# Regrouping the weight conversion's calls on ScalarE and GpSimd in a fused attention and feed-forward kernel

## The chip, the cores and the metric

The kernel runs on one core of one Trainium2 chip. The metric is the device time of one launch in microseconds (us), taken as the median of several runs. Times inside the launch come from one execution recorded by the hardware profiler; they are counted from the start of its span.

## What is computed

The inputs q, k, v have 8 batches, 8 heads, 576 rows and 64 columns. The feed-forward weights `w_ch1` (512 x 2048) and `w_ch2` (2048 x 512) come out of the set-up as 64-bit floats, since they are multiplied by a 64-bit scalar. The reference, cut to what matters:

```python
scores = scale * np.matmul(q, k.transpose(0, 1, 3, 2))          # scale = 1/8
thresh = np.max(scores, axis=-1, keepdims=True) - tau
scores = np.where(scores >= thresh, scores, -1000000000.0)
attn = np.exp(scores - np.max(scores, axis=-1, keepdims=True))
attn = attn / (np.sum(attn, axis=-1, keepdims=True) + 1e-09)
x = heads_to_columns(np.matmul(attn, v))                        # (8, 576, 512)
xn = (x - mean(x)) / np.sqrt(var(x) + 1e-06) * g_ln
out = x + np.maximum(xn @ w_ch1, 0.0) @ w_ch2
```

## The kernel before, in words

**Slots and quarters.** The attention is cut into 72 slots, nine for each batch. A slot n computes the scores of one pair of heads and half of the rows (one slot of each batch takes the rows left over), their maxima on VectorE (L436), thresholds on GpSimd (`thr`, L440), exponentials on ScalarE (L450) and masked weights on VectorE (L457), and turns the weights so that they can be multiplied with v. In slots 0 to 5 the turning is done by TensorE against a diagonal (`turn_weights`). From slot 6 (`FIRST`) on, GpSimd divides the weights (L473), VectorE turns them in blocks of 32 (`turn_blocks`, L541 and L547), and SyncE sends them through a scratch tensor in DRAM (`scr`, L554 and L558) and back into `em` (L568, L572) during the next slot. The product with v (L616) uses `em` near the end of that next slot.

**Feed-forward groups.** There are 16 groups of 288 tokens. Group 0 starts in slot 6. Its steps come from a generator, and `second_part(n, i)` issues a number of them in each of the four quarters i of a slot n, by a running account of steps owed. In `first_part` each of the 16 row blocks d is four products into a PSUM tile of the tag `ff`, of which there are two buffers, followed by a relu on ScalarE (L814) that frees the buffer. A block is issued only when the weights that it needs are ready (`conversion.ended`). After one of the first relus come the square of xc (L821) and three additions on GpSimd (L823) for the variance. `second_plain` holds the second product of group 0, with copies (L853) in the place of the relus. Later groups use weights that are ready.

**The conversion of the weights.** The class `Weights` turns the 64-bit words into 32-bit floats in 32 chunks of 128 x 512; chunks 0 to 15 belong to `w_ch1`, the rest to `w_ch2`. Each chunk passes these steps:

- `fetch`: SyncE loads the raw 64-bit words into a piece of some room that is free at that time (L257).
- `begin`: two VectorE instructions make the upper bits (L273, L277). They read the high word of each pair.
- the "low" conversion: ScalarE converts the low word in place (L283).
- the "square": ScalarE squares the high word, read as a float, in place (L286). It must wait until `begin` has read that word.
- `carry`: GpSimd adds the converted low word (L296). `carry_all` does this for all begun chunks, the last one first.
- `mask`: VectorE sets tiny values to zero by the square (L302), and the piece is free again.
- `scale`: for chunks 0 to 15, GpSimd multiplies by g_ln (L312).

Two chunks are begun at the end of slot 0, and one at each of two places in slots 1 to 5. The table `BEGUN` sets this: chunks 12 to 14 are begun in the second quarter of slot 6 and 15 to 17 in the third; 18 and 19, then 20 to 22 in slot 7; 23 to 25, then 26 and 27, and 28 at the end in slot 8; 29 and 30, then 31 in slot 9.

**What sets the order.** The order of each engine's queue is the order of the calls in the program, which is written by hand (`manual_schedule`); each engine works through its queue in order. ScalarE's two instructions for a chunk are not issued by `begin`. They are kept in the list `on_scalar`, low and square alternating. `flush(1)` after each relu takes one from the list, and `flush()` in `carry_all` takes all that are left.

In a slot's order, the places that matter are, in the main loop: `mask_all` and `begin_to(masks_at)` (L1128, L1129); for slots up to 5 `carry_all` and `scale_all` (L1130 to L1132); the second quarter of feed-forward steps (L1134); `carry_all` and `scale_all` (L1135, L1136); `weights` (L1138); `mask_all` and `begin_to(behind_at)` (L1143, L1144); the third quarter (L1146); `carry_all` (L1147); the turning (L1151 or L1155). A further `scale_all` stands in `exponentials` (L446), between the two thresholds of the next slot.

Of the kernel before, what the change touches and what calls it, by code (L numbers as in the profile page):

```python
# [13 lines left out]
AF = mybir.ActivationFunctionType  # L14
# [4 lines left out]
def kernel(  # L19
# [31 lines left out]
    nc = tc.nc  # L51
# [125 lines left out]
    class Weights:  # L177
# [13 lines left out]
        def __init__(self):  # L191
            self.chunks = [
                (w1_sb[i][:, c : c + WC], w_ch1[i * 128 : (i + 1) * 128, c : c + WC], i)
                for c in range(0, DF, WC)
                for i in range(NK)
            ] + [
                (
                    w2_sb[:, m, d : d + 4].rearrange("p d c -> p (d c)"),
                    w_ch2[d * 128 : (d + 4) * 128, m * 128 : (m + 1) * 128].rearrange(
                        "(d p) c -> p d c", p=128  # L200
                    ),
                    None,
                )
                for m in range(NK)
                for d in range(0, ND, 4)
            ]
            self.n1 = NK * (DF // WC)
            self.fetched = self.begun = self.carried = self.masked = self.scaled = 0
            self.raw, self.ticks, self.on_scalar = {}, 2, []
            flat = lambda t: t.rearrange("p a b -> p (a b)")  # L210

            x_room = ffn.tile([128, NK, TOK], F32, tag="x", bufs=3, name="x_room")
            y_room = ffn.tile([128, NK, TOK], F32, tag="sq", bufs=1, name="y_room")
            stage = self.stage = consts.tile([128, 8, WC], F32, name="stage")

            n1 = self.n1
            self.free = []  # L220
            for t, n, before in (
                (w2_sb.rearrange("p m d c -> p (m d) c"), ND // 2, lambda p: n1 + 2 * p - 6),
                (hidden, 4, lambda p: 10),
                (x_room, 1, lambda p: 2 * n1),
                (y_room, 1, lambda p: 2 * n1),
                (stage, 4, lambda p: 2 * n1),
            ):
                for p in range(n):
                    self.free.append((before(p), -1, flat(t)[:, p * 2 * WC : (p + 1) * 2 * WC]))
# [37 lines left out]
        def begin(self):  # L267
            i = self.begun
            assert all(self.raw[j][0] + 6 > i or self.raw[j][0] == 10 for j in range(self.masked, i))
            self.begun += 1  # L270
            hi = self.words(i, U32)[:, :, 1]
            au = self.chunks[i][0].bitcast(U32)
            nc.vector.tensor_scalar(  # L273
                out=au, in0=hi, scalar1=3, scalar2=0x3FFFFFFF,
                op0=ALU.logical_shift_left, op1=ALU.bitwise_and,
            )
            nc.vector.scalar_tensor_tensor(  # L277
                out=au, in0=hi, scalar=0xC0000000, in1=au,
                op0=ALU.bitwise_and, op1=ALU.bitwise_or,
            )  # L280
            low, low_in, top = self.words(i, I32), self.words(i, U32), self.words(i, F32)[:, :, 1]
            self.on_scalar += [
                lambda: nc.scalar.activation(  # L283
                    low[:, :, 0], low_in[:, :, 0], func=AF.Copy, scale=2.0**-29
                ),
                lambda: nc.scalar.activation(top, top, func=AF.Square),  # L286
            ]

        def flush(self, most=99):
            while self.on_scalar and most:  # L290
                most -= 1
                self.on_scalar.pop(0)()

        def carry(self, i):
            ai = self.chunks[i][0].bitcast(I32)
# [34 lines left out]
        def carry_all(self):  # L330


            self.flush()
            for i in reversed(range(self.carried, self.begun)):
                self.carry(i)
            self.carried = self.begun

        def mask_all(self):
            while self.masked < self.carried:
                self.mask()  # L340

# [194 lines left out]
    def turn_blocks(b, s, es):  # L536


        et = att.tile([128, NB, 128], F32, tag="et", bufs=1, name="et")
        if s == HP:  # L540
            nc.vector.transpose(  # L541
                et.rearrange("p n (u c) -> p u n c", u=HP),
                es.rearrange("p u (n c) -> p u n c", c=32),
            )
        else:
            for h in range(2):
                nc.vector.transpose(  # L547
                    et[:, :, 64 * h : 64 * h + 64].rearrange("p n (j c) -> p j n c", j=2),
                    es[:, 2 * h : 2 * h + 2].rearrange("p j (n c) -> p j n c", c=32),
                )  # L550
        scr = dram.tile([4, S, 128], F32, tag="scr", name="scr")
        if b == 0:
            for a in range(4):
                nc.sync.dma_start(  # L554
                    out=scr[a].rearrange("(n r) x -> r n x", r=32), in_=et[32 * a : 32 * a + 32]
                )
            return scr
        nc.sync.dma_start(  # L558
            out=scr.rearrange("a (r n) x -> (a r) (n x)", r=32),
            in_=et.rearrange("p n x -> p (n x)"),  # L560
        )
        return scr
# [231 lines left out]
    def first_part(g):  # L794
# [6 lines left out]
        for d in range(ND):  # L801
# [10 lines left out]
                if c < NK - 1:  # L812
                    yield 1, 1
            nc.scalar.activation(hidden[:, d], p1, func=AF.Relu)  # L814
            conversion.flush(1)
            next(sums_of, None)
            yield 2, 1
            if sq is None and d and (plain or part > 1 or d == ND // 2 - 1):
# [188 lines left out]
    def at_quarter(n, i, fn, *args):  # L1007
        later_calls.setdefault((n, i), []).append((fn, args))
# [84 lines left out]
    for n in range(NS):  # L1093
# [33 lines left out]
            run_all(aside)  # L1127
        conversion.mask_all()  # L1128
        conversion.begin_to(masks_at)  # L1129
        if n <= HP + 1:  # L1130
            conversion.carry_all()
            conversion.scale_all()  # L1132
        run(n, 1)
        second_part(n, 1)  # L1134
        conversion.carry_all()  # L1135
        conversion.scale_all()  # L1136
        blocks_go = by_blocks(n)
        diags = weights(es, thr, blocks_go)  # L1138
        run_all(aside)
# [1 line left out]
        if n < SLOTS:  # L1141
            run_all(stores)
        conversion.mask_all()  # L1143
        conversion.begin_to(behind_at)  # L1144
        run(n, 2)
        second_part(n, 2)  # L1146
        conversion.carry_all()  # L1147
        box = []
        if blocks_go:
            conversion.fetch(3, wait=0)  # L1150
            scr = turn_blocks(b, s, es)  # L1151
            at_quarter(n + 1, 0, lambda b=b, s=s, scr=scr, box=box: box.append(fetch(b, s, scr)))
        else:

            made = turn_weights(s, es, diags)  # L1155
            for i, at in enumerate(
                (-1, -1, 0, 0)
            ):
                if i < 3:
                    at_quarter(n + 1, at, next, made)  # L1160
                else:
                    at_quarter(n + 1, at, lambda made=made, box=box: box.append(next(made)))
# [17 lines left out]
        second_part(n, 3)  # L1180
        conversion.begin_to(end_at)
        conversion.carry_all()
        run_all(aside)
        drip({nc.vector: 2, nc.gpsimd: 0})
    while later_calls or queue or aside or stores or drops:
# [39 lines left out]
```

## Time and profile before

| what | value |
|---|---|
| median of 3 runs | 1354.78 us (1354.15 to 1355.54) |
| the profiled execution | 1355.44 us |
| its span | 1353.6 us, 40455 instructions |
| TensorE busy | 1320.4 us, 98% |
| VectorE busy | 877.9 us, 65% |
| GpSimd busy | 630.3 us, 47% |
| ScalarE busy | 458.8 us, 34% |
| waits of ScalarE's squares (L286) for `begin` (L277), first 270 us | 10.3 + 8.8 + 4.6 + 3.3 + 1.1 us by the room of the raw words |
| waits of GpSimd's additions (L296) for the low conversions (L283), first 270 us | 16.9 + 8.2 + 7.8 + 7.0 us |

Busy times of the engines overlap, and an engine's idle time matters only where another engine waits for what comes behind it. A line of the timeline gives start, length, engine, line, operation, output and input, the number of instructions, and in brackets how long the engine stood idle before it and what ended that. The conversion's work lies in the first 172 us of the span; slots 0 to 5 take the first 78 us or so, slots 6 to 9 some 16 to 24 us each.

### The profile page before, as it was taken

How to read it: one execution, taken by the hardware profiler on the slowest of the kernel's cores; microseconds unless marked ns; L12 is line 12 of the kernel's file. 1: busy time of each engine (PE TensorE's matmuls, PEld its weight loads, DVE VectorE, ACT ScalarE, POOL GpSimd, SP SyncE). 2: the span in 40 equal slices, each digit the busy share in tenths (PEclk: the TensorE clock that was granted, in tenths of full speed). 3: DMA queues.
4: the chain of work that ended last, by engine and by line, in shares of the span. 5: the costliest groups of instructions: out<-in, count | busy, mean ns of one | idle time of the engine just before them, and what ended most of it. 6: DMA issues, size and time to landing. Idle time of an engine off the chain costs nothing.

```text
span 1353.6 us, 40455 instructions
## 1 busy us (share of the span) xinstructions
PE 1320.4 (98%) x17400; PEld 993.8 (73%) x17400; DVE 877.9 (65%) x1544; ACT 458.8 (34%) x995; POOL 630.3 (47%) x836
## 2 busy tenths in 40 slices
PE   8989899999999999999999999999999999999997
PEld 6754557869687786967778696876868677686957
DVE  7979977666755675666766667556756667666112
ACT  4865432232323323232333323233232323323120
POOL 3566655445444344444534545444444445335312
PEclk9999999999999999999999999999999999999999
DMA  8916884457644675437744476446764376343211
GB/s 159 290 39 185 216 210 148 176 155 188 182 146 146 191 194 174 151 129 192 194 141 159 138 199 182 151 146 186 188 181 152 119 195 185 125 159 128 85 18 20
DMA packets 335299, 213.94 MB, mean 158 GB/s; under 512 B 247376, under 2 KB 292688, under 8 KB 327056
## 3 DMA queue, kind: packets, MB, share of 16 engines
q1 hardware_dynamic: 329008, 210.46, 53.3%
q8 instruction: 137, 2.24, 0.7%
q10 hardware_dynamic: 5952, 0.74, 0.4%
q0 software_dynamic: 160, 0.15, 0.1%
q14 instruction: 42, 0.34, 0.1%
HBM read 124.00 MB, written 87.29 MB: 156 GB/s over the span
## 4 chain that ended last, share of the span: by engine, by line
PE 87%; SPq 1%; issue 1%; DMA 1%; DVE 0%; POOL 0%; ACT 0%; POOLq 0%; ACTq 0%; DVEq 0%
PE p L101 36%; PE seg L101 31%; PE sc L422 9%; PE sc L616 8%; PE sc L626 2%; PE var L101 1%; PE mean L101 1%; DMA em<-scr 0%; SPq L554 0%; ACT part L902 0%; SPq L118 0%; DMA k_in<-in_k_dram 0%; DVE et L547 0%; POOL w L296 0%; POOL out_dram L745 0%
## 5 line engine op out<-in xcount | busy, mean ns | idle before, releaser
L101 PE MATMUL p<-xc,w 128*64 128x288 f32 x4096 | 519.4, 409 | 9.8 <-ACT part L902 4.6
L101 PEld LDWEIGHTS p<-xc,w 128*64 128x64 f32 x4096 | 287.2, 137 | 219.6 <-issue 14.8
L436 DVE TENSOR_REDUCE neg<-sc 128x2 f32<-128x1152 f32 x144 | 188.6, 1351 | 282.4 <-PE sc L422 282.4
L473 POOL TENSOR_SCALAR e<-e,den 128x576 f32<-128x576 f32 x264 | 209.5, 805 | 133.6 <-DVE den L462 133.6
L101 PE MATMUL seg<-hidden,w 128*64 128x144 f32 x3840 | 247.9, 287 | 0.0
L101 PEld LDWEIGHTS seg<-hidden,w 128*64 128x64 f32 x3840 | 234.9, 137 | 11.5 <-issue 8.5
L457 DVE SCALAR_TENSOR_TENSOR e<-sc,thr,e 128x576 f32<-128x576 f32 x288 | 222.3, 809 | 17.3 <-POOL thr L440 11.6
L440 POOL TENSOR_SCALAR thr<-neg,low_sb 128x2 f32<-128x2 f32 x144 | 41.6, 289 | 377.7 <-DVE neg L436 376.8
L814 ACT ACTIVATE hidden<-p 128x288 f32<-128x288 f32 x256 | 106.2, 415 | 295.6 <-PE p L101 295.6
L450 ACT ACTIVATE e<-sc,neg 128x576 f32<-128x576 f32 x288 | 197.5, 754 | 2.4 <-DVE neg L436 2.4
L547 DVE STREAM_TRANSPOSE et<-e 128x1152 f32<-128x1152 f32 x118 | 161.1, 1372 | 14.3 <-POOL e L473 13.7
L422 PE MATMUL sc<-kT,qT 64*64 64x384 f32 (+3 forms) x2048 | 139.4, 403 | 3.1 <-DVE e L457 1.9
L616 PE MATMUL sc<-em,v_in 128*64 128x128 f32 (+1 forms) x2368 | 130.9, 264 | 5.2 <-DMA em<-scr 3.7
L616 PEld LDWEIGHTS sc<-em,v_in 128*64 128x64 f32 x2368 | 123.4, 138 | 14.0 <-DVE o L728 2.5
L101 PE MATMUL seg<-hidden,stage 128*64 128x144 f32 x1920 | 123.3, 286 | 0.0
L101 PEld LDWEIGHTS seg<-hidden,stage 128*64 128x64 f32 x1920 | 117.6, 137 | 2.9 <-issue 2.9
L639 ACT COPY x<-sc 128x128 f32<-128x128 f32 x120 | 31.6, 265 | 243.8 <-PE sc L422 176.0
L887 POOL TENSOR_TENSOR hidden<-hidden 128x576 f32<-128x576 f32 x60 | 84.8, 1428 | 52.0 <-ACT hidden L814 42.4
L422 PEld LDWEIGHTS sc<-kT,qT 64*64 64x64 f32 x2048 | 76.0, 133 | 44.2 <-issue 21.4
L902 ACT COPY part<-seg 128x288 f32<-128x288 f32 x74 | 29.8, 403 | 190.6 <-PE seg L101 190.1
L887 DVE TENSOR_TENSOR hidden<-hidden 128x576 f32<-128x576 f32 x60 | 51.2, 887 | 51.5 <-PE seg L101 48.5
L823 POOL TENSOR_TENSOR hidden<-hidden 128x288 f32<-128x288 f32 x48 | 38.9, 810 | 54.7 <-ACT hidden L821 52.2
(132 smaller groups left out, 1088.2 us busy)
## 6 DMA issues: line engine op xcount, KB each, us to landing
scr<-et SPq DMA_DIRECT2D x63, 1152.0 KB, 5.0
em<-scr SPq DMA_DIRECT2D x63, 1024.0 KB, 5.7
out_dram<-ot SPq DMA_DIRECT2D x248, 36.0 KB, 3.6
q_in<-in_q_dram SPq DMA_DIRECT2D x120, 72.0 KB, 2.5
er<-scr SPq DMA_DIRECT2D x132, 64.0 KB, 5.1
k_in<-in_k_dram SPq DMA_DIRECT2D x116, 72.0 KB, 2.8
v_in<-in_v_dram SPq DMA_DIRECT2D x28, 256.0 KB, 5.4
w<-in_moe_w_ch_dram SPq DMA_DIRECT2D x11, 512.0 KB, 6.5
```

The costliest lines, as they stand in the source:

```text
L101: nc.tensor.matmul(out[r], lhsT=lhsT[:, r], rhs=rhs, **flags)
L422: nc.tensor.matmul(sc[h][64 * i : 64 * i + 64, at : at + n], lhsT=ql[r] if s == HP else qT[r, half, j * 128 + 64 * i : j * 128 + 64 * i + 64],
L436: nc.vector.tensor_reduce(out=neg[:, i], in_=pairs[h], axis=AXL.X, op=ALU.max, negate=True,)
L440: nc.gpsimd.tensor_scalar(out=thr[:, i], in0=neg[:, i], scalar1=-1.0, scalar2=low_sb, op0=ALU.mult, op1=ALU.add,)
L450: nc.scalar.activation(es[:, i], blocks[i], func=AF.Exp, bias=neg[:, i : i + 1])
L457: nc.vector.scalar_tensor_tensor(out=es[:, i], in0=blocks[i], scalar=thr[:, i : i + 1], in1=es[:, i], op0=ALU.is_ge, op1=ALU.mult, accum_o ...
L473: nc.gpsimd.tensor_scalar(out=es[:, i], in0=es[:, i], scalar1=den[:, i : i + 1], scalar2=1.0, op0=ALU.mult, op1=ALU.mult,)
L547: nc.vector.transpose(et[:, :, 64 * h : 64 * h + 64].rearrange("p n (j c) -> p j n c", j=2), es[:, 2 * h : 2 * h + 2].rearrange("p j (n c) ...
L616: nc.tensor.matmul(dst[64 * h : 64 * h + 64], lhsT=vt[:, h, c, :], rhs=pick(em[:, 2 * j : 2 * j + 2, c], h), start=c == 0 and first, stop= ...
L814: nc.scalar.activation(hidden[:, d], p1, func=AF.Relu)
L823: nc.gpsimd.tensor_tensor(out=sq[:, 0], in0=sq[:, 0], in1=sq[:, c], op=ALU.add)
L887: eng.tensor_tensor(out=out[at], in0=in0[at], in1=in1[at], op=op)
```

## The change

The list `on_scalar` is split in two, `lows` and `squares`. `flush` becomes `give_scalar`, which issues from either list.

- `carry_all` issues all pending lows, then the additions. `mask_all` issues all pending squares first.
- After a relu, one pending square is issued, and only in the second quarter.
- In every slot, `carry_all` and `scale_all` now stand ahead of the second quarter's steps, and the remaining squares behind them.
- From slot 6 on, `scale_all` is also called after the second `mask_all`.
- After the third quarter all pending lows are issued. In slots 0 to 5 the additions and squares follow at once. From slot 6 on `turn_blocks` comes first, then the squares, then the additions.
- At the end of a slot squares follow `carry_all`.

```diff
@@ Weights
-            self.raw, self.ticks, self.on_scalar = {}, 2, []
+            self.raw, self.ticks, self.lows, self.squares = {}, 2, [], []
...
-            self.on_scalar += [
-                lambda: nc.scalar.activation(
-                    low[:, :, 0], low_in[:, :, 0], func=AF.Copy, scale=2.0**-29
-                ),
-                lambda: nc.scalar.activation(top, top, func=AF.Square),
-            ]
-
-        def flush(self, most=99):
-            while self.on_scalar and most:
+            self.lows.append(lambda: nc.scalar.activation(
+                low[:, :, 0], low_in[:, :, 0], func=AF.Copy, scale=2.0**-29
+            ))
+            self.squares.append(lambda: nc.scalar.activation(top, top, func=AF.Square))
+
+        def give_scalar(self, calls, most=99):
+            while calls and most:
                 most -= 1
-                self.on_scalar.pop(0)()
+                calls.pop(0)()
...
         def carry_all(self):
-            self.flush()
+            self.give_scalar(self.lows)
             for i in reversed(range(self.carried, self.begun)):
                 self.carry(i)
             self.carried = self.begun
 
         def mask_all(self):
+            self.give_scalar(self.squares)
             while self.masked < self.carried:
                 self.mask()
@@ first_part
             nc.scalar.activation(hidden[:, d], p1, func=AF.Relu)
-            conversion.flush(1)
+            if part == 1:
+                conversion.give_scalar(conversion.squares, 1)
@@ main loop
         conversion.mask_all()
         conversion.begin_to(masks_at)
-        if n <= HP + 1:
-            conversion.carry_all()
-            conversion.scale_all()
+        conversion.carry_all()
+        conversion.scale_all()
         run(n, 1)
         second_part(n, 1)
-        conversion.carry_all()
-        conversion.scale_all()
+        conversion.give_scalar(conversion.squares)
         blocks_go = by_blocks(n)
         diags = weights(es, thr, blocks_go)
...
         conversion.mask_all()
+        if n >= FIRST:
+            conversion.scale_all()
         conversion.begin_to(behind_at)
         run(n, 2)
         second_part(n, 2)
-        conversion.carry_all()
+        conversion.give_scalar(conversion.lows)
+        if n < FIRST:
+            conversion.carry_all()
+            conversion.give_scalar(conversion.squares)
         box = []
         if blocks_go:
             conversion.fetch(3, wait=0)
             scr = turn_blocks(b, s, es)
+            conversion.give_scalar(conversion.squares)
+            conversion.carry_all()
...
         second_part(n, 3)
         conversion.begin_to(end_at)
         conversion.carry_all()
+        conversion.give_scalar(conversion.squares)
```

## The prediction

> **What bounds the kernel now.** I read the span by stages first. The rows give, per stretch, its length, the busy time and count of PE, weight loads, VectorE, ScalarE and GpSimd, the granted clock and the DMA share.
>
> ```profile
> core 0: us, PE busy (x) PEld busy (x) DVE busy (x) ACT busy (x) POOL busy (x), PEclk, DMA share, GB/s
> ...
> 82.00:104.00 22.00, 19.19 (x160) 11.16 (x160) 13.81 (x25) 12.07 (x23) 14.28 (x13) 0.93 0.00 1
> 104.00:124.00 20.00, 18.78 (x206) 11.26 (x208) 17.87 (x29) 9.77 (x21) 14.32 (x14) 0.99 0.82 225
> 124.00:146.00 22.00, 18.52 (x158) 10.88 (x152) 20.11 (x35) 10.91 (x22) 13.68 (x14) 0.92 0.69 169
> 146.00:171.00 25.00, 21.25 (x205) 13.21 (x204) 23.69 (x39) 10.84 (x19) 17.03 (x17) 0.93 0.86 218
> ...
> 300.00:1300.00 1000.00, 995.67 (x13340) 760.68 (x13338) 629.82 (x1101) 307.38 (x680) 451.85 (x618) 1.00 0.54 161
> ```
>
> From 171 us on TensorE is the bound: 995.67 us of 1000. The conversion of the 32 weight chunks ends there, so the edited calls lie wholly in slots 0 to 9. In slots 6 to 9 (82 to 171 us) TensorE still stands idle at times, and the granted clock falls to 0.92 to 0.93. Time won there moves everything behind it forward. So I followed the chain of waits back from 171 us:
>
> ```profile
> 138.03 2.56 POOL w L296 x2
> ...
> 147.50 2.63 DVE et L547 x2
> ...
> 150.15 0.33 SPq L554
> ...
> 159.59 5.55 DMA em<-scr
> ...
> 165.28 2.66 PE sc L616 x28
> ```
>
> The last matmuls with a wait, at 165.28, get their `em` from slot 8's turning. VectorE ended that at 150.13; SyncE's queue and the landing follow it. VectorE is busy nearly without a break from 106.74 (slot 7's maxima) to 150, and what feeds it is GpSimd's additions (L296). The timeline of slot 6, by engines, shows where the first loss starts:
>
> ```profile
> 92.68 0.40 ACT L814 ACTIVATE hidden<-p 128x288 f32<-128x288 f32 x1
> 99.56 0.68 ACT L286 ACTIVATE w<-w 128x512 f32<-128x512 f32 x1 [6.48 <-DVE w L277]
> 100.14 0.40 ACT L814 ACTIVATE hidden<-p 128x288 f32<-128x288 f32 x1
> ...
> 91.44 3.79 POOL L296 TENSOR_TENSOR w<-w,w 128x512 int32<-128x512 int32 x3 [1.16 <-ACT w L283]
> ...
> 96.42 5.38 POOL L473 TENSOR_SCALAR e<-e,den 128x576 f32<-128x576 f32 x4
> ...
> 95.27 2.31 DVE L302 SCALAR_TENSOR_TENSOR w<-w,w 128x512 f32<-128x512 f32 x3 [7.95 <-POOL w L296]
> ...
> 96.50 1.63 PE L101 MATMUL p<-xc,w 128*64 128x288 f32 x12
> 100.58 3.65 PE L101 MATMUL p<-xc,w 128*64 128x288 f32 x16 [2.46 <-ACT hidden L814]
> ```
>
> The low-word conversions of chunks 12 to 14 run between relus and squares, so GpSimd adds only from 91.44, and VectorE waits 7.95 us to mask. Then a square (L286) waits 6.48 us for VectorE's next begin, the relu at 100.14 stands behind it, and TensorE waits 2.46 us for its bank. It then takes 3.65 us for 16 matmuls that take 2.16 at 106.62.
>
> **What the Trainium skill says.** "Perfetto Trace Analysis", Tensor Engine Instruction: ScalarE, VectorE and GpSimd are strict FIFO. The trace agrees: that relu did nothing for 6.48 us. "GPSIMD Engine Reference", 1. Specifications: GpSimd shares its SBUF interfaces with VectorE and contends when VectorE has two SBUF inputs. The trace agrees: a mask (L302) takes 0.68 us alone and 1.06 to 1.14 beside a GpSimd scaling or division; a division (L473) 0.745 alone and about 1.35 here. "TensorE: Matmul & The Clock Gate", What's actually happening: an idle window of about 3.4 us halves the clock, and as long a busy one restores it. Here a shorter gap, 2.46 us, goes with the slow 16 matmuls; the measured price, 1.5 us on top of the gap, is what I use.
>
> **The change, part by part.** No instruction and no DMA is added or removed: there remain 32 low conversions, 32 squares, 32 additions, 16 scalings. The matmuls per quarter stay too: I worked through the issue loop's sums for both orders and no quarter is cut short by a weight that is not ready. SyncE's order stays. What moves, by my reading of the order:
>
> 1. Slot 0's end. Two chunks: low, low, square, square in place of low, square, low, square. The second low starts at 19.54 in place of 20.11, and GpSimd's additions, which begin with the second chunk, 0.57 earlier. Behind them stands the scaling of q, for which VectorE waits:
>
> ```profile
> 22.11 1.30 POOL L296 TENSOR_TENSOR w<-w,w 128x512 int32<-128x512 int32 x1
> ...
> 23.40 0.74 POOL L355 TENSOR_SCALAR qk_room<-qk_room,scl_sb 128x576 f32<-128x576 f32 x1
> ...
> 24.18 0.45 DVE L382 STREAM_TRANSPOSE qT<-qk_room 128x256 f32<-128x256 f32 x1 [1.15 <-POOL qk_room L355]
> ```
>    From there VectorE works on to the scores of slot 2, so **0.55 us** won. Slots 1 to 5 convert one chunk at a time; there the square only moves behind the copies of x, and ends just before the diagonals need ScalarE (slot 2: about 40.9 against 41.15; slot 5: 73.95 against 73.92). Cost 0 to 0.05 us; the cover is that wait for `den`.
>
> 2. Slot 6. Lows 12, 13, 14 follow the relu at 86.18 and run 86.49 to 88.2, ahead of the 1.16 us square of xc. Additions at 88.37 in place of 91.44. GpSimd's queue is then: 3 additions 3.79, scaling 11 1.22, the three adds of L823 2.56 (they now stand behind; nobody needs them before 104), 4 divisions 3.3 to 5.4, scalings 12 to 14 newly here 2.1 to 3.0, 3 additions 3.8. Sum: 17 to 20 us, so the additions of chunks 15 to 17 end at 105.5 to 108, taken 107.0 (106.3 now).
>    ScalarE: no square stands ahead of a relu in this second half, so the bank wait of 2.46 and the 1.5 us of slow clock go, and 0.32 at 92.27. TensorE reaches slot 7's scores about 4.2 us sooner, at 100.4. The relu after the lows ends about 89.8, just when its bank is wanted (89.97).
>
> 3. Slot 7. VectorE's turning of slot 6 ends about 102.2 (104.88 now), maxima run 102.4 to 105.0. What is late next is GpSimd: masks 15 to 17 wait for the additions, 107.05 in place of 109.28; they run without the scalings beside them, 1.95 us in place of 2.60. So begin 18 starts at 109.0 in place of 111.88, **2.9 us** sooner, and VectorE works without a break to the turning of slot 7: weights, root, masks, begins, turning, all 2.9 sooner (ending 124.9). Added waits: square 18 stands behind a relu and waits for begin 18, square 19 for begin 19 (111.1); the relu behind them runs at 111.7, and TensorE wants its bank at 111.6, a new gap of about 0.5. Scaling 15 at 113.7 to 114.4 then holds the last quarter of that product, 0.8 (0.47 now). TensorE is 3.4 sooner there; at slot 8's first relus (130.52 now, behind maxima and exponentials) it is again at VectorE's 2.9.
>
> 4. Slot 8. Additions 23 to 25 start with begin 25's end, 134.7, in place of 138.03, 0.4 us after the end of begin 25 (137.6): another **0.3 us**. Turning 8 ends about 3.2 sooner, if the first two parts do. SyncE is free 3.2 us before that turning now, and moves forward with turning 7. So `em` lands 3.2 sooner, and TensorE's 165.28 becomes 162.1. In slot 9 nothing more is found.
>
> From 171 on TensorE has no slack to lose this in. Sum: 0.55 + 2.9 + 0.3, less 0.15 for the small costs, is **3.6 us**. The profiled execution took 1355.44 us (span 1353.6 and 1.8 around it), 0.66 above the median of the runs, 1354.78; against it 1351.8, against the median 1351.2.
>
> Bounds of what the trace doesn't show: GpSimd's chain in slot 6 from 17 to 20 us puts masks 15 at 105.5 to 108, a gain of 4.4 to 1.9 in parts 2 and 3. Additions under VectorE's masks are not priced at slot 6; one beside such work (L668) took 1.17 us for 0.73, so L823 may cost 1.2 more, inside that range. Loss is not excluded by this: see the second rival.
>
> **The rivals.** A measurement of this kernel can tell about 0.2%, 2.7 us, from no change.
> - *Lost in the queue of GpSimd*, 0.20: contention makes slot 6's queue as long as it can be, masks 15 to 17 start where they do now, and `em` of slot 8 lands at nearly the same time. For it: TensorE's gain of slot 6 counts only if VectorE keeps up, and GpSimd is 14.28 of 22 us busy there. Gain 0.5 to 2: 1353.5.
> - *A square takes the relu's place in slot 7, and it is slower*, 0.20: squares 18 and 19 stand between relus, behind begins, masks, additions, scalings. If the additions end after 110.7 (3.7 later than I take), the relu comes after 115.5, TensorE idles over 3.9 us at its bank (now at 115.97), the clock falls, and the 1.5 us or more of slow matmuls come twice, with VectorE late for the turning: about 3 us lost, 1357.8. Against it: even all contended prices give 110.2.
> - *More waits go*, within the faster case: GpSimd's uncontended prices all along, and 4.4 + 0.85: 1349.5. The idle stretches of TensorE from 82 to 171 add up to 11.2 us (0.32, 2.46, 0.75, 0.47, 2.02, 1.43, 1.44, 2.31), which bounds any gain.
> - That the change does not do what it says is partly so: only slots 6 and 7 have relus in the second quarter with squares pending, so just squares 12 and 18 stand behind such relus; slots 8 and 9 have none.
>
> **How the numbers follow.** Forecast 0.60, 1351.2, its own range 1349.5 to 1352.0. Rival one 0.20, within 0.2%; rival two 0.20, slower. Low end 1349.6; the high end takes in rival one and the near part of rival two, 1355.6.
>
> **What would show it.** Right: no L286 ahead of a relu with 6.48 us idle in slot 6, additions at about 88.4, masks 12 near 92.2, no 2.46 us gap, masks 15 near 107, turning 7 ending near 125, the late `em` matmuls near 162. Wrong: relus of slot 7 behind squares with TensorE idle over 2 us, or turning 8 not moved.

## The result and the profile after

The changed kernel takes **1349.67 us** (median of 7 runs, 1349.3 to 1350.62); the kernel before takes 1353.89 us beside it (7 runs, 1351.46 to 1355.54). The ratio is 0.997, with a 95% interval of 0.9959 to 0.9982: 4.2 us less, somewhere from 2.4 to 5.5. The profiled execution took 1349.3 us with a span of 1347.5, against 1355.44 and 1353.6; this pair lies 6.1 us apart, 1.9 us more than the medians, so that much is particular to these two executions. Lines L282 to L310 of the changed kernel are the conversion (low L282, square L285, addition L294, mask L300, scaling L310); the relu is now L813, the turning L546, the em matmuls L615.

First the stages, one row each of the kernel before and of the changed one for the stretch that holds slots 6 to 9, and one of the rest of each, with the columns of the prediction's first fence:

```profile
78.00:172.00 94.00, 81.81 (x780) 49.27 (x780) 80.45 (x135) 46.40 (x89) 61.23 (x60) 0.95 0.57 147
172.00:1250.00 1078.00, 1073.07 (x14234) 808.01 (x14228) 710.83 (x1244) 342.83 (x755) 500.71 (x689) 1.00 0.56 166
```

```profile
78.00:172.00 94.00, 84.40 (x839) 51.00 (x836) 84.89 (x139) 49.73 (x95) 63.95 (x65) 0.98 0.61 161
172.00:1250.00 1078.00, 1073.07 (x14254) 809.55 (x14252) 708.46 (x1241) 341.97 (x754) 500.05 (x686) 1.00 0.57 166
```

In the same 94 us TensorE now gets 839 matmuls done in place of 780, and the granted clock is 0.98 in place of 0.95. From 172 us on its busy time is the same to the hundredth. The mean's matmuls of the next feed-forward group come at 171.36 in place of 177.31, and from there to the end of the span it is 1176.1 us and 1176.3. So the gain is made before that point, in slots 6 to 9, and neither added to nor lost later.

The timeline of slot 6 after the change, by engines (the lines that answer to the prediction's third fence):

```profile
86.92 1.80 ACT L282 ACTIVATE w<-w 128x512 int32<-128x512 uint32 x3
...
98.38 0.76 ACT L285 ACTIVATE w<-w 128x512 f32<-128x512 f32 x1 [1.86 <-DVE w L277]
...
101.79 0.73 ACT L813 ACTIVATE hidden<-p 128x288 f32<-128x288 f32 x2
...
106.41 0.42 ACT L813 ACTIVATE hidden<-p 128x288 f32<-128x288 f32 x1
...
88.80 3.82 POOL L294 TENSOR_TENSOR w<-w,w 128x512 int32<-128x512 int32 x3 [8.45 <-ACT w L282]
...
93.25 3.67 POOL L823 TENSOR_TENSOR hidden<-hidden 128x288 f32<-128x288 f32 x3
96.89 4.89 POOL L472 TENSOR_SCALAR e<-e,den 128x576 f32<-128x576 f32 x4
...
92.66 3.60 DVE L300 SCALAR_TENSOR_TENSOR w<-w,w 128x512 f32<-128x512 f32 x3 [4.91 <-POOL w L294]
...
103.64 2.58 DVE L435 TENSOR_REDUCE neg<-sc 128x2 f32<-128x1152 f32 x2
107.54 0.69 DVE L300 SCALAR_TENSOR_TENSOR w<-w,w 128x512 f32<-128x512 f32 x1 [1.32 <-POOL w L294]
...
102.28 2.16 PE L101 MATMUL p<-xc,w 128*64 128x288 f32 x16
...
106.88 10.15 PE L101 MATMUL p<-xc,w 128*64 128x288 f32 x68 [1.96 <-ACT hidden L813]
```

The three lows now run in one piece, the additions start at 88.80 in place of 91.44, VectorE's wait at mask 12 is 4.91 in place of 7.95, and the gap of 2.46 us is gone. Two relus still stand behind squares that wait for VectorE (squares from 98.38, relus at 101.79), but TensorE has `er` and score matmuls to do until 102.27 and takes up the next product at 102.28 without a wait. But TensorE's lead is handed back a little later: at 106.88 it waits 1.96 us for a relu again. That relu stands on ScalarE behind slot 7's first exponentials, these wait for the maxima of slot 7, and the maxima (103.64) stand on VectorE behind slot 6's turning (101.09 to 103.71). Slow matmuls follow this gap: 68 take 10.15 us, and 68 at full speed take 8.47 at 128.03.

The chain of waits, back from slot 10:

```profile
134.51 2.56 POOL w L294 x2
...
143.99 2.63 DVE et L546 x2
...
146.64 0.33 SPq L553
...
155.95 4.82 DMA em<-scr
...
160.90 1.75 PE sc L615 x28
...
166.91 4.52 PE p L101 x36
171.42 0.64 PE mean L101 x3
```

These are the same links as before. Slot 8's turning starts 3.5 us sooner, the `em` transfer takes 4.82 in place of 5.55, and the late `em` matmuls come 4.4 us sooner and run at full speed (1.75 us in place of 2.66).

### The profile page after: what moved, and what is told of

It is laid out like the page before. It is cut to its first block, busy times and chain, and to the rows that moved or that the text cites. A ratio compares the mean times of both kernels' runs of the same rounds, so it can differ in the third digit from the quotient of the medians.

```text
span 1347.5 us, 40451 instructions
## 1 busy us (share of the span) xinstructions
PE 1316.5 (98%) x17400; PEld 992.2 (74%) x17400; DVE 878.3 (65%) x1544; ACT 460.4 (34%) x995; POOL 630.4 (47%) x836
## 4 chain that ended last, share of the span: by engine, by line
PE 87%; SPq 1%; issue 1%; DMA 1%; DVE 0%; POOL 0%; ACT 0%; POOLq 0%; ACTq 0%; DVEq 0%
PE p L101 36%; PE seg L101 31%; PE sc L421 9%; PE sc L615 8%; PE sc L625 2%; PE mean L101 1%; PE var L101 1%; DMA em<-scr 0%; SPq L553 0%; ACT part L902 0%; SPq L118 0%; DVE et L546 0%; POOL w L294 0%; DMA k_in<-in_k_dram 0%; SPq L142 0%
## 5 line engine op out<-in xcount | busy, mean ns | idle before, releaser
L813 ACT ACTIVATE hidden<-p 128x288 f32<-128x288 f32 x256 | 106.2, 416 | 299.5 <-PE p L101 299.5
L546 DVE STREAM_TRANSPOSE et<-e 128x1152 f32<-128x1152 f32 x118 | 161.1, 1373 | 14.3 <-POOL e L472 13.7
L615 PE MATMUL sc<-em,v_in 128*64 128x128 f32 (+1 forms) x2368 | 130.0, 263 | 5.2 <-DMA em<-scr 3.8
L615 PEld LDWEIGHTS sc<-em,v_in 128*64 128x64 f32 x2368 | 122.7, 137 | 14.1 <-issue 3.2
L823 POOL TENSOR_TENSOR hidden<-hidden 128x288 f32<-128x288 f32 x48 | 40.0, 833 | 46.9 <-ACT hidden L821 44.4
```

Of the source, the lines that this page charges most:

```text
L546: nc.vector.transpose(et[:, :, 64 * h : 64 * h + 64].rearrange("p n (j c) -> p j n c", j=2), es[:, 2 * h : 2 * h + 2].rearrange("p j (n c) ...
L615: nc.tensor.matmul(dst[64 * h : 64 * h + 64], lhsT=vt[:, h, c, :], rhs=pick(em[:, 2 * j : 2 * j + 2, c], h), start=c == 0 and first, stop= ...
L823: nc.gpsimd.tensor_tensor(out=sq[:, 0], in0=sq[:, 0], in1=sq[:, c], op=ALU.add)
```

## The experiments

The kernels were timed in three groups (e1 to e4, e5 to e8, the rest), each beside runs of the kernel before, whose medians were 1353.83 (39 runs), 1353.98 (33) and 1354.42 (37). e1 and e2 edit the kernel before, the others the changed kernel. The ratio is that to the kernel before; it is worked out together with its interval and can differ by up to 0.1% from the quotient of the medians. Where a profile is read, it is that of one execution.

| kernel | median, us | ratio (95% interval) |
|---|---|---|
| changed kernel | 1349.67 | 0.9970 (0.9959 to 0.9982) |
| e1, new order in slots 0 to 5 alone | 1352.96 | 0.9996 (0.9988 to 1.0004) |
| e2, before, third-quarter relus free | 1351.51 | 0.9981 (0.9975 to 0.9988) |
| e3, third quarter as before | 1350.54 | 0.9970 (0.9961 to 0.9980) |
| e4, without the new scaling call | 1350.04 | 0.9970 (0.9958 to 0.9981) |
| e5, additions ahead of the turning | 1350.18 | 0.9972 (0.9965 to 0.9980) |
| e6, gap of slot 7 filled with matmuls | 1349.60 | 0.9969 (0.9958 to 0.9979) |
| e7, values late in slot 9 | 1349.40 | 0.9969 (0.9960 to 0.9977) |
| e8, values late in slots 8 and 9 | 1349.10 | 0.9966 (0.9954 to 0.9978) |
| e14, e8 with chunk 31 begun in slot 10 | 1356.89 | 1.0019 (1.0013 to 1.0026) |
| e16, e8 with the sum early | 1349.21 | 0.9964 (0.9951 to 0.9977) |
| e18, changed kernel with chunk 31 without VectorE | 1351.17 | 0.9968 (0.9959 to 0.9977) |
| e19, e8 with chunk 31 without VectorE | 1349.31 | 0.9961 (0.9947 to 0.9975) |

### Which part brings the gain: e1 to e5

**e1** gives the kernel before the new grouping in slots 0 to 5 and leaves the rest.

```diff
 def carry_all(self):
-    self.flush()
+    if self.ticks_early:
+        lows, squares = self.on_scalar[0::2], self.on_scalar[1::2]
+        self.on_scalar[:] = squares
+        for fn in lows:
+            fn()
+    else:
+        self.flush()
@@ behind the second quarter, behind the third quarter's carry_all, and at the slot's end
+        if n < FIRST:
+            conversion.flush()
@@ at the slot's end
+        conversion.ticks_early = n + 1 < FIRST
```

> The kernel before with the new order in slots 0 to 5 alone (lows, additions, then squares), slots 6 to 9 as before. The prediction's step 1 expects 0.55 us less. My theory after the trace of the changed kernel: the first begin of slot 1 then waits for its raw chunk's landing instead, so 0 (within 0.5 us), and the first begin of slot 6 is not earlier than the 80.7 us of the kernel before by more than 0.3. Rival (the early slots carry the gain): 3 us or more less.

No gain can be told: 0.9996 (0.9988 to 1.0004, from 1.6 us less to 0.5 more, so that 0.55 less is not excluded; 3 us less is). In its trace VectorE's wait for the scaling of q in slot 1 is gone altogether, yet the maxima ahead of it had waited 0.54 us for the scores. The wait for raw words that the theory named is not in this trace: slot 1's first begin comes at 26.92 without one. Slot 6's first begin stands at 81.98, after 80.70 before and 81.13 in the changed kernel. The early slots don't carry the gain.

**e2** takes ScalarE's conversions out from between the relus of the third quarter of the kernel before.

```diff
             nc.scalar.activation(hidden[:, d], p1, func=AF.Relu)
-            conversion.flush(1)
+            if part != 2:
+                conversion.flush(1)
```

> The kernel before, but no conversion is issued between the relus of the third quarters of slots 6 and 7: they all follow the last relu there. GpSimd's order is untouched. My theory: TensorE loses the 2.46 us gap and its slow matmuls in slot 6, slot 7's maxima start at the end of the turning (104.9) in place of 106.74, and VectorE's chain, masks 15 at about 107.5 in place of 109.28, hands on 1.8 us: the whole is 1.5 to 2.5 us faster, about half of the change. Rival (relus behind squares are the whole of it): 4 us faster. Rival (only GpSimd's early additions count): 0.

0.9981 (0.9975 to 0.9988), 2.6 us of the 4.2. Its profiled execution was the slowest of its 21 (1353.98, median 1351.51), so the trace shows the order of things and not the usual time. The gap in slot 6 shrinks from 2.46 to 1.02 and slot 7's maxima start right behind the turning. The gap in front of the next relus is there as in the changed kernel, from TensorE's timeline of e2:

```profile
103.47 2.16 PE L101 MATMUL p<-xc,w 128*64 128x288 f32 x16 [1.02 <-ACT hidden L814]
...
108.14 8.21 PE L101 MATMUL p<-xc,w 128*64 128x288 f32 x52 [2.02 <-ACT hidden L814]
```

**e3** puts the third quarter back: lows and squares by turns behind its relus, the additions ahead of the turning.

```diff
             if part == 1:
                 conversion.give_scalar(conversion.squares, 1)
+            else:
+                conversion.give_pairs(1)   # low, square, low, square
@@ main loop, behind the third quarter
-        conversion.give_scalar(conversion.lows)
+        conversion.give_pairs()
+        conversion.carry_all()             # and none behind turn_blocks
```

> The changed kernel, with the third quarter as before: a low or a square by turns behind each relu, the rest and the additions ahead of the turning. Second quarter and the extra scaling stay changed. My theory: a relu of slot 6 stands behind square 15 again, but begin 15 is 1.2 us sooner, TensorE idles 1 to 1.5 us there, has a lead to lose, and VectorE's chain moves by 0.1 to 0.5 us only: 3 to 4 us faster than the kernel before, within 1 us of the changed one. Rival (relus behind squares are the whole of it): no faster than before by more than 1 us.

By the ratio the whole gain is still there: 0.9970 (0.9961 to 0.9980); by the medians 3.3 us of it are. A relu waits behind a square again, and TensorE stands idle for 1.39 us at 99.72, but GpSimd's additions of chunks 12 to 14 start at 89.12 and begin 18 comes at 109.69, nearly as in the changed kernel (88.80 and 109.36). The new order of the third quarter is therefore not needed, or for no more than can be told. With e1 and with e4 below, what remains to carry the gain is that the lows run in one piece *ahead of the second quarter* and GpSimd starts early; no run has this part alone. e2 leaves GpSimd's order as it was and brings a part of the gain, e3 leaves e2's part out and loses nothing that can be told: the two parts overlap and don't add up.

**e4** leaves out the new `scale_all` behind the second `mask_all`; **e5** puts the additions ahead of the turning, the squares still behind it.

```diff
@@ e4
-        if n >= FIRST:
-            conversion.scale_all()
@@ e5
+            conversion.carry_all()
             scr = turn_blocks(b, s, es)
             conversion.give_scalar(conversion.squares)
-            conversion.carry_all()
```

> The changed kernel without the extra scaling after the second masks; chunks 12 to 14 are scaled between slot 7's thresholds as before. My theory: GpSimd adds chunks 15 to 17 2.0 us sooner (ends near 105.5), masks 15 to 17 start right behind slot 7's maxima (106.2 in place of 107.5) but beside the scalings, 0.4 us longer each, so begin 18 at 109.0 to 109.4: within 0.5 us of the changed kernel either way. Rival (the earlier scaling itself is needed, since products wait for scaled weights): slower than the changed kernel by 1 us or more.

> The changed kernel with the later additions issued ahead of the block turning instead of behind it (squares still behind it). GpSimd has no instruction of its own in the turning, so its queue is the same; my theory: the same time as the changed kernel, within 0.1%, about 4 us faster than before. Rival (the place behind the turning is worth something): 1 us or more slower than the changed kernel.

Both make no difference that can be told (1350.04 and 1350.18). In e4 masks 15 to 17 start at 106.06 without a wait and begin 18 at 108.45, 0.9 us sooner than in the changed kernel, and slot 8's turning 0.6 us sooner (143.36 against 143.99), but the late `em` matmuls come at 161.05 against 160.90, and slow (28 in 3.21 us): the lead does not reach TensorE in this execution.

### What the slow matmuls cost: e6

**e6** repeats the variance product five times in group 0, so that TensorE has work while slot 7's relu is late.

```diff
-                product(var, lhsT=avg_sb, rhs=sq[:, 0], start=True, stop=True)
+                for _ in range(5 if plain else 1):
+                    product(var, lhsT=avg_sb, rhs=sq[:, 0], start=True, stop=True)
```

> The changed kernel; the variance product of group 0 is issued five times in a row instead of once (each overwrites the last with the same values), to keep TensorE at work in the 1.96 us gap of slot 7. Theory (the clock falls because of the gap, and TensorE is off the path there): the products behind the gap take 8.5 us in place of 10.15, TensorE waits the more for slot 8's relus, VectorE's turnings do not move, and the end is the same within 0.5 us. Rival (TensorE's work in slot 7 sets the end): 1.5 us or more faster than the changed kernel. Rival (the slow matmuls have another cause): still 10.15 us.

TensorE's timeline of e6:

```profile
103.55 2.60 PE L101 MATMUL var<-hidden,avg_sb 128*64 128x288 f32 x20
106.15 2.16 PE L101 MATMUL p<-xc,w 128*64 128x288 f32 x16
108.95 6.56 PE L101 MATMUL p<-xc,w 128*64 128x288 f32 x52 [0.64 <-ACT hidden L832]
```

The gap of 1.96 us and the slow matmuls behind it are gone, and the end is the same, 1349.60. The trace has slow matmuls in slot 8 in their place (28 in 3.09 us behind a gap of 2.25), so the time alone would not settle it. VectorE's chain does: from slot 6's first begin to slot 8's turning it takes 62.90 us here. In the eight other traces of this order through slot 7 (the changed kernel, e5, e7, e8, e14, e16, e18, e19) it takes 62.86 to 62.99, in four of them with slow matmuls behind slot 7's gap and in four without. At that place VectorE sets the pace, and the slow matmuls fall into time that TensorE has to spare.

### What holds the end of the stage: e7, e8, e14, e16, e18, e19

**e7** and **e8** issue the values of the slot before (the `em` matmuls) behind the last quarter's four products, so that TensorE has them to do while `em` lands.

```diff
-        run(n, 3)
+        if n not in (8, 9):      # e7: (9,)
+            run(n, 3)
...
         second_part(n, 3)
+        if n in (8, 9):
+            run(n, 3)
```

> The changed kernel; in slot 9 alone the product of slot 8's weights with v stands behind the last quarter's four feed-forward products instead of ahead of them. Theory (TensorE waits in slot 9 for em of slot 8, and that wait sets the end): 2.1 us of products fill a wait of 2.7 us, so about 2 us faster than the changed kernel, 6 us faster than before. Rival (that wait is slack of something else): no difference.

> As the one with slot 9 alone, and in slot 8 as well (the wait there is 2.5 us). Theory (the landing of slot 8's em, at the end of VectorE's chain, takes back what TensorE gains earlier): the same as with slot 9 alone, within 0.5 us. Rival (each wait of TensorE counts by itself): 2 us faster again.

Both missed: 1349.40 and 1349.10, where about 2 us less than the changed kernel were expected. TensorE's timeline of e8 shows the next thing that is late:

```profile
160.82 1.75 PE L615 MATMUL sc<-em,v_in 128*64 128x128 f32 x28 [2.26 <-DMA em<-scr]
162.50 0.45 PE L625 MATMUL sc<-er,v_rest 64*64 64x128 f32 x8
162.77 2.12 PE L421 MATMUL sc<-kT,qT 64*64 64x384 f32 x32
164.82 4.59 PE L101 MATMUL p<-hidden,w 128*64 128x288 f32 x36
171.09 0.71 PE L101 MATMUL mean<-sum,avg_sb 128*64 128x288 f32 x4 [1.68 <-POOL sum L667]
```

The 16 matmuls of the last quarter are out of the way, but the mean of the next group then waits 1.68 us for GpSimd's sum. That sum needs slot 8's values in `x`, whose copy on ScalarE waits 3.91 us for slot 10's maxima; and those stand on VectorE behind chunk 31's landing (162.68), its begin, slot 9's turning (164.67) and mask 31. In the changed kernel the weight load of the same mean waits 0.44 us for the sum. By these traces two chains end there almost together, `em` and VectorE's. The last four kernels were to test that.

**e14** lets VectorE begin chunk 31 only in slot 10; **e16** puts the copy and the sum ahead of slot 10's maxima. Both start from e8.

```diff
@@ e14: BEGUN
-        ... (26, 29, 29), (31, 32, 32),
+        ... (26, 29, 29), (31, 31, 31), (32, 32, 32),
@@ e16
-            at_quarter(n, "copy", copy, 0)
-            at_quarter(n, "copy", add)
+            at_quarter(n, -1 if n == SLOTS + 1 else "copy", copy, 0)
+            at_quarter(n, -1 if n == SLOTS + 1 else "copy", add)
```

> Slots 8 and 9 as in e8 (values behind the last quarter's products), and chunk 31 begun by VectorE in slot 10, behind slot 10's maxima, in place of ahead of slot 9's turning. Theory (VectorE's chain sets the end of the stage: landing of chunk 31, begin 31, turning 9, maxima of slot 10, x copy, sum, mean): turning 9 starts at the end of the divisions, about 163.3 in place of 164.7, maxima of slot 10 at 166.8 in place of 168.5, the mean's matmuls without a wait at 169.4; but begin 31 then stands ahead of the subtraction xc, so only 0.8 us of the 1.7 arrive: about 0.8 us less than e8 (1348.3). Rival (the em transfer of slot 8 alone sets the end): the same as e8, 1349.1, within 0.4 us.

> e8 with the copy of slot 8's values into x and the addition into sum ahead of slot 10's maxima, not between them. Theory: the sum then stands behind the residual addition (ends 169.54) alone, starts 0.8 us sooner, the mean's matmuls too, and about 0.7 us of it reaches the end: 1348.4. Rival (VectorE's subtraction xc comes at 173.45 whatever the mean does, since VectorE has work without a break until then): 1349.1, no gain.

e14 missed: 0.8 us less than e8 were expected, and it takes 7.8 us more by the medians (7.2 by the ratios). Half of its theory stands in TensorE's timeline, and so does what it overlooked:

```profile
169.63 0.66 PE L101 MATMUL mean<-sum,avg_sb 128*64 128x288 f32 x4
170.12 0.66 PE L101 MATMUL p<-hidden,w 128*64 128x288 f32 x4
178.18 4.09 PE L101 MATMUL p<-hidden,w 128*64 128x288 f32 x16 [7.40 <-DVE w L300]
```

The mean has no wait and comes at 169.63 (169.4 expected). But the last product of `second_plain` needs chunk 31, and its mask now stands on VectorE behind xc and slot 10's weights: 7.40 us of idle TensorE, and slow matmuls after it (16 in 4.09 us in place of some 2.1). A chunk that is moved out of a busy engine's way has a reader, and the theory had not placed it.

e16 gained nothing on e8 (1349.21). In its profile chunk 31 landed later, VectorE waited 1.22 us for it, and xc came at 174.26 with the product on xc at 174.83; so the rival's reading (xc comes when VectorE gets there) fits, but this one trace does not exclude that the landing hid a gain.

**e18** and **e19** take chunk 31 off VectorE, in the changed kernel and in e8. One copy on ScalarE stands in for the two begin instructions, and the mask is left out, so the last row block of `w_ch2` does not hold the right numbers.

```diff
+            if i == 31:
+                nc.scalar.activation(self.chunks[i][0], self.words(i, F32)[:, :, 1], func=AF.Copy)
+            else:
                 nc.vector.tensor_scalar(...)            # begin, L273
                 nc.vector.scalar_tensor_tensor(...)     # begin, L277
@@ mask: only for i < 31
```

> The changed kernel, in which chunk 31 is made without VectorE: one ScalarE copy in place of its two begin instructions, and its mask left out (so the last row block of w_ch2 is not the right numbers). It takes some 2.4 us of work and the wait for the landing out of VectorE's chain in slots 9 and 10. Theory (in the changed kernel two chains end together: em of slot 8, and VectorE's): the mean's wait of about 0.4 us for the sum goes, nothing more: 0.3 us less than the changed kernel, 1349.4 against 1349.7. Rival (VectorE's chain alone sets the end): 1.5 us less or more, 1348.

> e8 with chunk 31 made without VectorE as in e18 (its mask left out, the last row block of w_ch2 not the right numbers). Both chains are shortened. Theory (both end together): turning 9 starts at 163.3, maxima of slot 10 at 166.7, the mean at 169.4 without a wait, xc at 171.7: 1.5 to 1.7 us less than e8, about 1347.5; that is the gain that e7 and e8 missed. Rival (something else holds e7 and e8, after the mean): 1349, no gain.

VectorE's and TensorE's timelines of e19:

```profile
162.32 2.82 DVE L550 STREAM_TRANSPOSE et<-e 128x1152 f32<-128x1152 f32 x2
...
166.72 2.62 DVE L439 TENSOR_REDUCE neg<-sc 128x2 f32<-128x1152 f32 x2 [0.65 <-PE sc L425]
```

```profile
160.99 2.55 PE L619 MATMUL sc<-em,v_in 128*64 128x128 f32 x28 [1.97 <-DMA em<-scr]
163.47 0.71 PE L629 MATMUL sc<-er,v_rest 64*64 64x128 f32 x8
163.95 2.73 PE L425 MATMUL sc<-kT,qT 64*64 64x384 f32 x32
166.61 4.59 PE L101 MATMUL p<-hidden,w 128*64 128x288 f32 x36
171.02 0.66 PE L101 MATMUL mean<-sum,avg_sb 128*64 128x288 f32 x4
```

The waits went as the theory said: turning 9 at 162.32, maxima of slot 10 at 166.72 (now waiting for TensorE), xc at 171.72, the mean without a wait. Yet the mean comes at 171.02. The `em`, `er` and score matmuls behind the 1.97 us gap took 5.99 us in place of the 4.32 that e8 shows: 1.7 us of slow matmuls stand where the wait was, and the median is 1349.31. So e19's number speaks against a gain and its trace says why in that execution; that the other five runs lost their gain in the same way was not seen. e18's profile has slow matmuls at that place too (28 in 3.25 us after a gap of 2.33), and its 15 runs fall into two groups, 1348.9 to 1350.0 and 1351.2 to 1352.5, the profiled one (span 1349.4) in the upper. The lower group has its middle at 1349.5, where the changed kernel has its median (1349.67), so no gain from chunk 31 shows, against the 0.3 us that were expected; the rival's 1348 is not reached by any of the 15. Why the upper group is so frequent here was not found out. That two chains hold the end together is therefore not shown: none of the four kernels excludes that something else does.

None of these kernels beats the changed one by what can be told.

## Why the prediction was right, and where it was not

The forecast of 1351.2 us was 1.5 us above the result, on the right side and inside the range; 3.6 us less were forecast, and 4.2 less were measured between the medians. Of the 1.5 us, 0.9 is the kernel before, whose median was 1354.78 in three runs and is 1353.89 in seven. By the prediction's steps:

1. **Slots 0 to 5, 0.55 us: true in some executions only, and not in the profiled one.** The scaling of q did come sooner (VectorE waits 0.61 for it, 1.15 before), but in slot 1 VectorE then stands at the next begin until its raw words land:

```profile
26.58 0.45 DVE L273 TENSOR_SCALAR w<-hidden 128x512 uint32<-128x512 uint32 x1 [0.62 <-DMA hidden<-in_moe_w_ch_dram]
```

   A transfer was next in line, and the prediction named none. From slot 0's first begin to slot 6's it takes 63.26 us here and 63.09 in the kernel before. Five other traces of the changed kernel's early order (e4, e6, e7, e14, e18) have that wait too, 0.19 to 0.71 us, and take 62.81 to 63.32. The five without it (e3, e5, e8, e16, e19) take 62.50 to 62.53: there the 0.55 us is won. Whether it reaches the end can't be told (e1).

2. **Slot 6: the times came true, one reason did not.** Additions at 88.80 (88.37 predicted; the slot began 0.43 later), chunks 15 to 17 added by 107.5 (107.0). GpSimd's queue took 18.7 us, inside the 17 to 20. The three adds of L823 cost 3.67 in place of 2.56, which the bounds had allowed with 1.2. This fits what "GPSIMD Engine Reference", 1. Specifications, in the Trainium skill says of VectorE instructions with two SBUF inputs, and the price can be read here: one such add 0.85 us alone, 1.22 beside VectorE's masks, which at the same time take 1.20 in place of 0.68. TensorE's scores of slot 7 came at 100.15 (100.4). The step had said that no square would stand ahead of a relu in this half of the slot. Squares 15 to 17 do: block 7's matmuls end at about 97.9 (reckoned from 28 matmuls in 3.56 us at 96.39), and its relu comes at 101.79. That cost nothing because the relu was done about when the scores were. (The prediction also gave the whole 6.48 us of ScalarE's wait to the relu at 100.14; its block's matmuls ended only at about 94.4, reckoned from the line at 92.27.)

3. **Slot 7: the size was right, the new gaps were not.** Begin 18 came at 109.36 (109.0), slot 7's turning ended at 124.86 (124.9). The gaps of 0.5 and 0.8 us behind squares and scaling 15 didn't appear. In their place came the 1.96 us at the exponentials, of which 0.75 stood there before. The step had slot 7's maxima at 102.4, as far ahead as TensorE; they came at 103.64, 3.1 us sooner than before where TensorE was 4.3 sooner, because VectorE's turning ended at 103.71 and not at 102.2. Of these 1.5 us, 0.5 is the later start of mask 12 (92.66, not 92.2); the rest is that the change puts masks 12 to 14 beside the adds of L823, where they took 3.60 us in place of 2.31. The step had also not asked which relu stands behind those maxima on ScalarE; by the strict order of its queue ("Perfetto Trace Analysis", Tensor Engine Instruction, in the Trainium skill, on which the prediction had drawn) that relu had to wait. Masks 15 to 17 had to wait for the additions even so (1.32 us), and e6 shows that the miss cost nothing.

4. **Slot 8: 0.3 us predicted on top of 2.9; 3.5 us in all measured at its turning.** At the late `em` matmuls 4.4 us were won, not 3.2. Of the difference, 0.3 lies at the turning, 0.2 in SyncE's queue, and 0.7 is a shorter transfer (4.82 us against 5.55). The traces speak for an accident of the execution and not for the change: the last landing of that transfer takes 4.7 us in e6 and 5.2 to 6.0 in the nine other traces of kernels made from the changed one.

5. **Slot 9, "nothing more": wrong in the profiled pair.** The execution before had slow matmuls behind its `em` gap (28 in 2.66 and 16 in 2.98 us, against 1.75 and 2.14). With the 4.4 us of step 4 that makes the 6.1 us between the two traces; the medians lie 4.2 apart, and such matmuls are slow in some executions only. Among the traces that leave slot 9's order alone they are slow in two of three with the order of before from slot 6 on (before and e2, not e1) and in three of six with the changed order there (e4, e5 and e18; not the changed kernel, e3 and e6). So these 1.7 us are not shown to come from the change. The slow lines stood in the trace before, and the prediction did not use them.

Against this pair, the sum of 3.6 us was 0.55 too high by step 1 and 1.2 too low by step 4, and it left out the 1.7 of slot 9. The mechanism was right: GpSimd's earlier additions move VectorE's chain, slot 8's turning by 3.5 us. That the forecast lies within 0.6 us of the measured difference is in part luck: it prices a trace of 1355.44, slower than the medians of the kernel before (1353.8 to 1354.4), and takes the slow matmuls of slot 6 in that trace as if every execution had them. The rival in which more waits go, 1349.5, has the better number, but not the mechanism: it took GpSimd's uncontended prices in slot 6, and the divisions (4.89 us for four) and the adds of L823 ran at contended ones. The rival in which GpSimd's queue takes the gain back is refuted by step 2's times; the one with squares in the relus' place in slot 7 by the absence of any such gap: TensorE works from 106.88 to 117.03 without a break. The last rival was true as far as it went: at none of the squares behind second-quarter relus does TensorE stand idle. e3 says more: the third quarter's regrouping, and with it the additions behind the turning (e5), isn't needed. The part that pays is, by elimination, `carry_all` ahead of the second quarter.

**How much is the shorter chain, and what stays open.** The time from slot 6's first begin to slot 8's turning separates the two for the traces at hand. It is 66.80 us in the kernel before. It is 65.17 in e1, which has the same order from slot 6 on and the same 2.46 us gap, but full-speed matmuls behind it; there slot 7's maxima wait 0.21 us for the scores, where the trace before has 1.85:

```profile
106.74 2.62 DVE L436 TENSOR_REDUCE neg<-sc 128x2 f32<-128x1152 f32 x2 [1.85 <-PE sc L422]
```

With the changed order it is 62.9. So about 2.3 us are won by the order itself, and 1.6 more where an execution of the kernel before has slow matmuls in slot 6. How often it has them, the single traces don't say: the kernel before scatters over 5 to 7.5 us (1351.5 to 1356.2 in 39 runs, 1351.0 to 1358.5 in 37), e2 over 3.2 in 21 runs, the changed kernel over 1.3 in 7.

## What to carry to other kernels

Ask first which engine feeds the engine that feeds the bound: here ScalarE's three short conversions, put in one piece ahead of the relus, let GpSimd start 2.6 us sooner, and by elimination that was enough to move TensorE's last wait. When a wait is taken away, list all the chains that end within a microsecond or two of it, the transfers among them; e7 and e8 each shortened what looked like the last wait and met the next at once. And when an operation is put off, find its reader first: e14 paid 7.4 us for one that was overlooked. Before a saving is priced from one trace, look at whether it recurs in other executions: the slow matmuls in slot 9 did in only some.

## What was not expected of the hardware

The matmuls behind an idle stretch are sometimes slow, mostly by 1.5 to 1.8 us in all (by 2 us in e14, behind 7.40 us), and the length of the stretch alone doesn't decide it:

| kernel, slot | gap, us | matmuls behind it | the same at full speed |
|---|---|---|---|
| before, 6 | 2.46 | 16 in 3.65 | 2.16 |
| e1, 6 | 2.46 | 16 in 2.16 | 2.16 |
| e1, 8 | 1.57 | 28 in 3.02, 16 in 2.62 | 1.75, 2.14 |
| e2, 7 | 2.02 | 52 in 8.21 | 6.53 |
| e4, 7 | 1.96 | 16 in 2.16 | 2.16 |
| before, 9 | 2.31 | 28 in 2.66, 16 in 2.98 | 1.75, 2.14 |
| e5, 9 | 2.26 | 28 in 3.06, 16 in 2.58 | 1.75, 2.14 |
| e8, 9 | 2.26 | 28 in 1.75 | 1.75 |
| e16, 9 | 2.75 | 28 in 1.75 | 1.75 |
| e18, 9 | 2.33 | 28 in 3.25 | 1.75 |
| e19, 9 | 1.97 | 28 in 2.55, 8 in 0.71, 32 in 2.73 | 1.75, 0.45, 2.12 |

"TensorE: Matmul & The Clock Gate", What's actually happening, in the Trainium skill gives an idle window of about 3.4 us for the clock to fall. Here gaps of 1.96 to 2.46 us were enough in some executions, and in e1 one of 1.57 that follows one of 0.92 with four matmuls between; one of 2.75 us was not enough in another. The measurements decide. The same section says that the window is free-running; whether where a gap falls in it is what decides here, no run settles.
